# The first expert product by Strassen's scheme, in an attention and mixture-of-experts kernel on one Trainium2 core

## The chip, the core and the metric

The kernel runs on one core of one Trainium2 chip. The core has a matrix engine (TensorE, "PE" in the profile, with its weight loads as "PEld"), a vector engine (DVE), a scalar engine (ACT), GpSimd (POOL) and a queue that issues transfers (SP). TensorE reads its operands from the on-chip memory SBUF and writes to PSUM, an accumulation memory of eight banks of 512 fp32 columns; DVE and ACT read both. Each engine runs its own instructions in the order in which the program emits them, and waits for others through semaphores.

The metric is the device time of one execution in microseconds (us), the median of several runs.

## The reference

The first half is attention over a window of 32 positions (for half of the heads with a dilation of 4). Its output, 4,608 tokens of 512 values, goes through a mixture of experts: each token is sent to its two best of eight experts, and an expert is two matrix products with a ReLU between them.

```python
N, D, E, F = (4608, 512, 8, 1024)
...
for e in range(E):
    for k in range(2):
        mask = top2[:, k] == e
        ...
        h = np.maximum(x[mask] @ w1[e], 0.0)
        out[mask] += top2_w[mask, k, None] * (h @ w2[e])
```

Everything is float32.

## The kernel before, in words

**Attention and routing** (the first 235 us of the profile) are emitted in fixed slots. While they run, each token's row is stored to the scratch tensor `xs`, its two experts are found (`gate`), and POOL scatters the token's number and weight into a table `tab` with one section per expert. Expert 0's section is filled from the start, so that its tokens are available first: `SPLITS` gives the rows that are complete after each quarter of the tokens (384 after the second, 896 after the third).

**Experts.** Each expert has a fixed capacity of 1,152 to 1,216 tokens (`CAPS`), in tiles of 128 (the last one of 64 or 32 tokens, or none). The tiles are grouped into three blocks of 3, 4 and 2 to 3 tiles (`BLS`): 384, 512 and 256 to 320 tokens. For each block, `up` computes the first product, 8 groups of 128 rows of the hidden layer, and `down` the second, tile by tile.

**Precision.** TensorE multiplies float32 operands in a rounded form (`F32R`). Each operand is therefore kept as a high part (its rounding, an ACT cast) and a low part (what is left, a DVE subtraction), and each product is three matmuls: high by high, high by low, low by high. So one row group of `up` is 4 slices of the 512 inputs times 3 = 12 matmuls (line 814) into one PSUM bank, with the block's tokens as the moving columns. After it, ACT takes the ReLU and the high part (L818, `hh`) and DVE the low part (L820, `hl`). A tile of `down` is 8 x 3 = 24 matmuls of 512 columns (L856); DVE scales it (L865, `y`), and POOL adds it to the output rows with an indirect DMA (L833). A last tile of at most 64 tokens is done with its high and low parts stacked in one operand (L850, L852), 16 matmuls.

**Tokens.** A tile's rows are gathered by POOL (four indirect DMAs, L766; two per tile for expert 0, L758), transposed on DVE (L783; for expert 0 on TensorE, L780), cast by ACT (L785) and subtracted by DVE (L786).

**Weights.** `stage_w1` and `stage_w2` load quarters of 512 KB through SP into two staging buffers; `split_w1` and `split_w2` are an ACT cast (L694, L707) and a DVE subtraction (L696, L709).

**The order** of all this work between the matmuls is a plan: `plan(t, f)` notes that `f` is due at time `t`, and `tick(cols)`, called after each group of matmuls, advances a clock by `cols / 2400` us (the columns just emitted) and emits what is due. Since each engine runs in emission order, this places the loads, casts and subtractions between the `hh` and `hl` operations. The order of blocks is written out per expert (first product of block 0, second product of the expert before's block 2, and so on), so that a product always has other work between it and its consumer. `pace()` emits a small POOL copy that waits for a recent `hh`, which holds the gathers behind it back.

## Time and profile before

| | us |
|---|---|
| median of 3 runs | 1053.06 |
| lowest and highest | 1047.64, 1053.71 |
| the profiled execution, first to last instruction | 1109.4 |
| of it, before the first matmul of the first product | 235.7 |
| of it, the eight experts on TensorE | 863.9 |
| of it, after the last matmul | about 10 |

The profile is that of one execution, with the profiler on; it is longer than the runs without it. Its page gives busy times per engine, the chain of waits and the costliest groups of instructions, and the trace behind it can be asked for the instructions of one engine in order of time (start, duration, engine, line, operation, output<-inputs, shape, count, and in brackets the idle time before it and what ended it), for busy times in windows, and for who waited for whom. Matmuls are pipelined: their durations overlap, so what one costs is read from the distance between starts.

### The profile page before, as it was taken

Reading aid. Unit: us, or ns where it says so; the run is one execution under the profiler, and the core shown is the slowest. Engines: PE = TensorE matmul, PEld = TensorE weight load, DVE = VectorE, ACT = ScalarE, POOL = GpSimd, SP = SyncE. Lnnn points to the kernel's source line nnn. Section 1 sums busy time; section 2 is a strip of 40 time slices with the busy share of each in tenths; the row PEclk is TensorE's granted clock in tenths of the full one; section 3 lists DMA queues with packets and bytes.
Section 4 is the critical chain, followed back from the end, with each engine's and each line's share of the span. In section 5 each row is a group of like instructions: output and inputs, shape, how many; then the busy total and the mean of one; then the engine's idle time right before and its main releaser. Section 6 shows DMA issues by size and latency. Waiting matters only on the chain. (4 is left out here: it accounts for less than half of the span.)

```text
span 1109.4 us, 18401 instructions
## 1 busy us (share of the span) xinstructions
PE 1015.0 (91%) x7278; PEld 853.6 (77%) x7279; DVE 463.9 (42%) x1060; ACT 319.8 (29%) x612; POOL 527.7 (48%) x723
## 2 busy tenths in 40 slices
PE   5896776686999899999999999999999999999996
PEld 3774655465779789878988898788978898888885
DVE  6773535644224444334433433434343344333221
ACT  6673433531113232222222222212231213222110
POOL 6004243356866545664635564455456455553112
PEclk9998887887999999999999999999999999999999
DMA  7798687465243432633353334333433443353123
GB/s 275 254 345 292 193 270 251 122 205 161 44 90 76 102 101 48 139 60 103 65 117 68 97 72 101 82 79 85 97 83 81 104 68 102 62 129 58 32 30 46
DMA packets 77530, 132.91 MB, mean 120 GB/s; under 512 B 29968, under 2 KB 39616, under 8 KB 76160
## 3 DMA queue, kind: packets, MB, share of 16 engines
q1 hardware_dynamic: 55088, 92.55, 26.3%
q0 software_dynamic: 22352, 39.15, 19.6%
q8 instruction: 58, 0.95, 0.4%
q14 instruction: 32, 0.26, 0.1%
HBM read 92.11 MB, written 39.54 MB: 119 GB/s over the span
## 5 line engine op out<-in xcount | busy, mean ns | idle before, releaser
L814 PE MATMUL up<-x,w1h 128*128 128x512 f32 (+4 forms) x1536 | 397.5, 345 | 8.8 <-DVE hl L820 5.8
L766 POOL DMA_INDIRECT g<-xs,ixi x258 | 264.5, 1025 | 84.5 <-issue 79.1
L814 PEld LDWEIGHTS up<-x,w1h 128*128 128x128 f32 x1536 | 272.7, 189 | 36.4 <-DVE hl L820 7.6
L814 PE MATMUL up<-x,w1l 128*128 128x384 f32 (+4 forms) x768 | 264.1, 344 | 1.8 <-DVE w1l L696 1.1
L856 PE MATMUL dn<-w2h,hh 128*128 128x512 f32 x576 | 226.7, 394 | 2.0 <-DVE y L865 1.3
L856 PE MATMUL dn<-w2h,hl 128*128 128x512 f32 x576 | 225.3, 391 | 1.1 <-issue 1.1
L856 PE MATMUL dn<-w2l,hh 128*128 128x512 f32 x576 | 225.5, 391 | 0.6 <-issue 0.6
L820 DVE SCALAR_TENSOR_TENSOR hl<-up,hh 128x384 fp32r<-128x384 f32 (+2 forms) x192 | 106.1, 556 | 228.0 <-ACT hh L818 177.1
L833 POOL DMA_INDIRECT out_rows<-y,ixs x67 | 107.8, 1609 | 189.3 <-DVE y L865 158.3
L818 ACT ACTIVATE hh<-up 128x384 fp32r<-128x384 f32 (+4 forms) x192 | 94.2, 498 | 274.7 <-PE up L814 193.9
L814 PEld LDWEIGHTS up<-x,w1l 128*128 128x128 f32 x768 | 145.7, 190 | 14.7 <-DVE w1l L696 1.8
L856 PEld LDWEIGHTS dn<-w2h,hh 128*128 128x128 f32 x576 | 109.0, 189 | 25.6 <-DVE y L865 2.4
L856 PEld LDWEIGHTS dn<-w2h,hl 128*128 128x128 f32 x576 | 108.8, 189 | 24.0 <-issue 1.1
L856 PEld LDWEIGHTS dn<-w2l,hh 128*128 128x128 f32 x576 | 109.0, 189 | 22.6 <-issue 0.8
L865 DVE TENSOR_SCALAR y<-dn,ixs 128x512 f32<-128x512 f32 x63 | 46.9, 748 | 143.4 <-PE dn L856 114.9
L785 ACT CAST x<-xr 128x512 fp32r<-128x512 f32 x67 | 40.5, 605 | 189.9 <-DVE xr L783 158.5
L619 POOL DMA_INDIRECT tab<-en,si x72 | 72.2, 1002 | 30.7 <-issue 16.4
L696 DVE TENSOR_TENSOR w1l<-ws,w1h 128x1024 fp32r<-128x1024 f32 x32 | 38.8, 1217 | 94.8 <-ACT w1h L694 61.6
L297 POOL COPY spacer<-hh 1x1 f32<-1x1 f32 x72 | 24.2, 336 | 102.0 <-ACT hh L818 101.7
L694 ACT CAST w1h<-ws 128x1024 fp32r<-128x1024 f32 x32 | 33.0, 1048 | 115.9 <-DMA ws<-in_moe_w 115.8
L786 DVE TENSOR_TENSOR x<-xr,x 128x512 fp32r<-128x512 f32 x67 | 44.7, 666 | 18.0 <-ACT x L785 15.9
L783 DVE STREAM_TRANSPOSE xr<-g 128x512 f32<-128x512 f32 x67 | 45.7, 682 | 0.0
(184 smaller groups left out, 856.0 us busy)
## 6 DMA issues: line engine op xcount, KB each, us to landing
ws<-in_moe_w SPq DMA_DIRECT2D x64, 512.0 KB
out_rows<-zero SPq DMA_DIRECT2D x38, 256.0 KB
vd<-in_vdl SPq DMA_DIRECT2D x24, 390.0 KB
vp<-in_vpl SPq DMA_DIRECT2D x16, 585.0 KB
qt<-in_qt SPq DMA_DIRECT2D x14, 576.0 KB
xs<-x SPq DMA_DIRECT2D x24, 256.0 KB
kt<-in_kd SPq DMA_DIRECT2D x16, 320.0 KB
g<-xs,ixi POOLq DMA_INDIRECT x258
```

The costliest lines, as they stand in the source:

```text
L619: ins = gpsimd.indirect_dma_start(out=tab, out_offset=bass.IndirectOffsetOnAxis(ap=si[:, kq, t:t + 1], axis=0), in_=en[:, kq, t], in_offse ...
L696: return lambda: vector.tensor_tensor(b, s, a.bitcast(F32), op=OP.subtract)
L766: gpsimd.indirect_dma_start(out=g[:, j], out_offset=None, in_=xq, in_offset=bass.IndirectOffsetOnAxis(ap=IX[e][1][:, r0 // 32 + j:r0 // 32 ...
L783: vector.transpose(xr[:, :, 0:rn].rearrange("p c (g t) -> p g c t", t=32), g[:, 0:n].rearrange("p g (c d) -> p g c d", d=32))
L785: scalar.copy(xh[:, :, o:o + rn], xr[:, :, 0:rn])
L786: return lambda: vector.tensor_tensor(xl[:, :, o:o + rn], xr[:, :, 0:rn], xh[:, :, o:o + rn].bitcast(F32), op=OP.subtract)
L814: tensor.matmul(p[:, 0:n], lhsT=a[:, 128 * f:128 * f + 128], rhs=b[:, kc, 0:n], start=(i == 0), stop=(i == 11))
L818: scalar.activation(hh[:, f, 0:n], p[:, 0:n], AF.Relu)
L820: vector.scalar_tensor_tensor(hl[:, f, 0:m], p[:, 0:m], 0.0, hh[:, f, 0:m].bitcast(F32), op0=OP.max, op1=OP.subtract)
L833: ins = gpsimd.indirect_dma_start(out=out, out_offset=bass.IndirectOffsetOnAxis(ap=sc[0:rn, t, 1:2], axis=0), in_=y[0:rn], in_offset=None, ...
L856: tensor.matmul(p[0:rn], lhsT=a[:, f, o:o + rn], rhs=b[:, f % 2], start=(i == 0), stop=(i == 23))
L865: vector.tensor_scalar(y[0:rn], p[0:rn], wsc, None, op0=OP.mult)
```

## The change

**The scheme.** Both operands of the first product are cut in two in both directions that matter: the 512 inputs into halves, the 1,024 hidden rows into pairs of groups, the block's tokens into halves of each tile. In place of 8 products of blocks, seven are computed, from sums of blocks of weights and sums of blocks of tokens, and the results are put together by additions (Winograd's form). Each product is 2 slices x 3 = 6 matmuls on half of a block's tokens.

**Tokens.** The two halves of each tile's tokens and of its inputs give eight slices, of which four sums are made (`xprep`) before the split: 14 slices of 64 tokens are cast and subtracted per tile (`xsplit`) instead of 4 of 128. Blocks are now two, of `NA = 5` tiles and of the rest (640 tokens, and 512 to 576); there is one buffer for the tokens of a block and one for its hidden layer. `SPLITS` becomes (0, 384, 640).

```diff
-        cuts = [0, 3, 7, len(tl_)]
-        BLS.append([(cuts[i], cuts[i + 1], 128 * cuts[i], min(cap, 128 * cuts[i + 1]) - 128 * cuts[i]) for i in range(3)])
+        BLS.append([(0, NA, 0, 128 * NA), (NA, len(tl_), 128 * NA, cap - 128 * NA)])
...
+    def xprep(e, t):
...
+        vector.tensor_tensor(b[:, 0], q[:, 0, :, 1], q[:, 0, :, 0], op=OP.subtract)
+        vector.tensor_tensor(b[:, 1], q[:, 1, :, 1], b[:, 0], op=OP.subtract)
+        vector.tensor_tensor(b4, q[:, 1, :, 0], b[:, 1], op=OP.subtract)
+        vector.tensor_tensor(q[:, 0, :, 1], q[:, 1, :, 1], q[:, 0, :, 1], op=OP.subtract)
...
+        scalar.copy(a[0], r)
+        def low():
+            vector.tensor_tensor(a[1], r, a[0].bitcast(F32), op=OP.subtract)
```

**Weights.** `kernel()` lays W1 out in blocks, so that one contiguous load of 256 KB brings the four blocks of one pair of row groups `j` and one slice `kk`; a ninth copy holds expert 0's in its other order of inputs. DVE makes four sums of 128 columns from it (`sums_w1`), and ACT and DVE split 7 blocks of 128 columns. W2 comes in eight loads of 256 KB instead of four of 512.

```diff
+    def sums_w1(w, j, kk, eng):
+        s = ST[w, j, kk]
+        a = s[:, 0:512].rearrange("p (i h f) -> p i h f", i=2, h=2)
+        b = s[:, 512:896].rearrange("p (o f) -> p o f", o=3)
+        eng.tensor_tensor(b[:, 0], a[:, 1, 0], a[:, 1, 1], op=OP.add)
+        eng.tensor_tensor(b[:, 1], b[:, 0], a[:, 0, 0], op=OP.subtract)
+        eng.tensor_tensor(b[:, 2], a[:, 0, 1], b[:, 1], op=OP.subtract)
+        eng.tensor_tensor(a[:, 1, 0], a[:, 0, 0], a[:, 1, 0], op=OP.subtract)
...
+        scalar.copy(t[:, 0, :, kk], s)
+        def low():
+            vector.tensor_tensor(t[:, 1, :, kk], s, t[:, 0, :, kk].bitcast(F32), op=OP.subtract)
```

**The first product.** A "row group" `j` is now a pair of 128 rows, and there are four per block. Row group `j`'s products are interleaved with the end of row group `i = j - 1`. `P` is a PSUM bank that accumulates four products in turn, `RQ` a pair of banks; `SU` and `M5` are SBUF copies ("snapshots") of what `P` and `RQ` hold midway, in buffers of their own (pool `ut`).

```diff
+        def mm(p, j, a, b, start):
+            w = W1[e, j]
+            for kk in range(2):
+                for i, (y, z) in enumerate(((0, 0), (0, 1), (1, 0))):
+                    tensor.matmul(p, lhsT=w[:, y, a, kk], rhs=x[:, z, SLOTS[b][kk], 0:N], start=start and kk == 0 and i == 0,
+                                  stop=kk == 1 and i == 2, skip_group_check=True)
+            tick(6 * N)
...
+        for j in range(5):
+            i = j - 1
+            if i >= 0:
+                vector.tensor_tensor(SU[i], SU[i], RQ[i], op=OP.add)
+                high(i, None, SU[i])
+            if j < 4:
...
+                mm(P[j], j, 0, 0, True)
+            else:
+                part()
+            if i >= 0:
+                low(i, None, SU.pop(i))
+            if j < 4:
+                scalar.copy(SU[j][:, 0], P[j])
+            if i >= 0:
+                mm(P[i], i, 2, 2, False)
+                vector.tensor_tensor(M5[i], M5[i], P[i], op=OP.add)
+                high(i + 4, 1, M5[i])
+            if j < 4:
+                mm(RQ[j][:, 1], j, 4, 4, True)
...
+            if i >= 0:
+                low(i + 4, 1, M5.pop(i))
+            if j < 4:
+                scalar.copy(M5[j], RQ[j][:, 1])
+                mm(RQ[j][:, 0], j, 1, 1, True)
+            if i >= 0:
+                mm(P[i], i, 3, 6, False)
...
+                high(i + 4, 0, P[i])
+            if j < 4:
+                mm(P[j], j, 5, 5, False)
...
+            if i >= 0:
+                low(i + 4, 0, P.pop(i))
+            if j < 4:
+                scalar.copy(SU[j][:, 1], P[j])
+                mm(RQ[j][:, 1], j, 6, 3, False)
```

`high` is an ACT ReLU, `low` a DVE subtraction (two for `SU`); for the small last tile each has a further small operation. `part()` emits a quarter of the first tile of the second product.

**The second product** runs block by block right after the first; its scaling moves from DVE to ACT.

```diff
-            vector.tensor_scalar(y[0:rn], p[0:rn], wsc, None, op0=OP.mult)
+            scalar.mul(y[0:rn], p[0:rn], wsc)
```

**The order.** The written plan with due times is replaced by generators that wait for each other: two for weights (one per slice `kk`, each: load, 5.5 us later the sums, 1.5 later the cast once the row group before is done with its buffer, 1.2 later the subtraction), one each for gathers, sums of tokens, splits of tokens and indices. Tokens of a block are split once the first product of the block before has been emitted. Gathers use three buffers instead of four and are preceded by a POOL memset in place of `pace()`.

```diff
+            for j in range(0 if e else 2, 4):
+                stage_w1(EID[e], e, j, kk)
+                yield now[0] + US_LOAD
+                sums_w1(e, j, kk, vector)
+                yield now[0] + 1.5
+                if e:
+                    yield lambda e=e, j=j: free1.get(j, -1) >= e - 1
+                low = split_w1(e, j, kk)
+                yield now[0] + 1.2
+                low()
+                yield now[0] + 0.2
...
     for e in range(E):
...
+        for bi in range(2):
+            t0, t1, _, n = BLS[e][bi]
+            while done.get((e, bi), 0) < t1 - t0:
+                tick(600)
+            begun.add((e, bi))
+            first = down_gen(e, bi, t0)
+            up(e, bi, n, first)
+            down(e, bi, first)
```

For expert 0 the first matmul of the first product comes after all five tiles of its first block have been emitted; its first two pairs of W1 row groups are loaded during attention, as before, and part of its W2 goes through gather buffers (`first_w2`).

More of the change, by code (lines that the diff above doesn't have):

```diff
@@ L257, in setup_c @@
         NR = ET // 16
-        free = [late["stage"].tile([128, FF], I32, name="free", tag="ws") for _ in range(2)]
+        free = [late["stage"].tile([128, 896], I32, name="free", tag="ws") for _ in range(2)]
         pr = free[0][:, 0:3 * NR].rearrange("p (a b) -> p a b", a=3)
@@ new lines, in attention_moe_kernel, with stage_w2, split_w2 @@
+    ready1, ready2 = {}, {}
+    def stage_w2(e, w, f, where=None):
+        s = ST[w, f] = (where or stage)()[:, 0:512]
+        sync.dma_start(s, row(w2, e)[128 * f:128 * f + 128])
+    def split_w2(w, f):
+        s = ST.pop((w, f))
+        a = late["wp2"].tile([128, DM], F32R, name=f"w2h{f}")
+        b = late["wp2"].tile([128, DM], F32R, name=f"w2l{f}")
+        scalar.copy(a, s)
+        def low():
+            vector.tensor_tensor(b, s, a.bitcast(F32), op=OP.subtract)
+            W2[w, f] = (a, b)
+        return low
@@ new lines, in first_w2, with gathers @@
+    def first_w2(fs):
+        held_g[0] += 1
+        for f in fs:
+            stage_w2(0, 0, f, lambda: gp_.tile([128, 4, 128], F32, name="g").rearrange("p a b -> p (a b)"))
+            yield now[0] + US_LOAD
+            low = split_w2(0, f)
+            yield now[0] + 0.9
+            low()
+            yield now[0] + 0.3
+        held_g[0] -= 1
+    def gathers():
+        for e in range(1, E):
+            yield lambda e=e: e in index
+            for t in range(len(TLS[e])):
+                yield lambda: held_g[0] < 3
+                gather(e, t)
+                got[e, t] = now[0]
+                held_g[0] += 1
+                yield now[0] + US_GATHER
@@ new lines, in indices, with rest_of_slots @@
+    def indices():
+        for e in range(1, E):
+            yield lambda e=e: (e - 1, 0) in begun
+            yield now[0] + (42 if e == 1 else 24)
+            new_idx(e)
+            idx_dma(e, 0, CAPS[e])
+            yield now[0] + (12 if e == 1 else 9)
+            idx_copy(e, 0, CAPS[e])
+            index.add(e)
+            yield now[0] + 0.5
+    def rest_of_slots():
+        n = 0
+        while backlog:
+            pace(n % 4 == 0)
+            backlog.pop(0)()
+            n += 1
+            yield 1
@@ new lines, in some_of_slots, with rest @@
+    def some_of_slots():
+        for i in range(min(6, len(backlog))):
+            pace(i == 0)
+            backlog.pop(0)()
+    experts[0] = True
+    for kk in range(2):
+        plan(0.1 + 0.6 * kk, lambda kk=kk: go(weights(kk)))
+    def rest():
+        gens.append(totals())
+        gens.insert(0, first_tiles(NA, len(TLS[0])))
+    gens.append(idx_late(list(gens), SPLITS[2], CAP, rest))
+    for i in range(36):
+        plan(i, some)
+    plan(2.5, some_of_slots)
+    plan(20, lambda: gens.append(rest_of_slots()))
```

437 lines of the change are left out of this document (236 added, 201 removed).

## The prediction

> **What bounds the kernel now.** I read the page's busy shares first, then the busy time of each engine expert by expert (cut where TensorE starts the first product of the next expert), then TensorE's timeline.
>
> ```profile
> span 1109.4 us, 18401 instructions
> PE 1015.0 (91%) x7278; PEld 853.6 (77%) x7279; DVE 463.9 (42%) x1060; ACT 319.8 (29%) x612; POOL 527.7 (48%) x723
> ```
>
> ```profile
> 235.70:365.25 129.55, 117.69 (x563) 99.58 (x562) 49.40 (x161) 25.25 (x47) 86.57 (x129) 0.93 0.46 118
> ...
> 570.12:675.24 105.12, 104.82 (x521) 90.49 (x520) 40.80 (x70) 24.15 (x41) 56.92 (x71) 1.00 0.39 86
> ...
> sum 863.90, PE 841.58 PEld 723.05 DVE 333.74 ACT 197.35 POOL 452.43; mean PE 105.20 PEld 90.38 DVE 41.72 ACT 24.67 POOL 56.55
> ```
>
> The columns after the length are PE, PEld, DVE, ACT and POOL busy, then the granted clock. From 235.70 us to the last matmul the eight experts take 863.90 us, and PE works in 841.58 of them: 22.3 us idle, of which 11.9 lie in expert 0 and 10.5 in experts 1 to 7. So this stage is bound by TensorE's work, at full clock after expert 0, and DVE (41.7 us of some 105 per expert) is cover with room. Busy shares of pipelined matmuls overstate, so I take the price of a matmul from the starts of successive ones:
>
> ```profile
> 601.35 0.63 PE L814 MATMUL up<-x,w1h 128*128 128x512 f32 x2
> ...
> 602.05 0.63 PE L814 MATMUL up<-x,w1h 128*128 128x512 f32 x2
> ...
> 675.24 0.51 PE L814 MATMUL up<-x,w1h 128*128 128x384 f32 x2
> ...
> 675.76 0.51 PE L814 MATMUL up<-x,w1h 128*128 128x384 f32 x2
> ```
>
> ```profile
> 331.12 0.45 PE L814 MATMUL up<-x,w1h 128*128 128x320 f32 x2
> ...
> 331.56 0.46 PE L814 MATMUL up<-x,w1h 128*128 128x320 f32 x2
> ...
> 640.07 0.43 PE L814 MATMUL up<-x,w1h 128*128 128x288 f32 x2
> ...
> 640.47 0.43 PE L814 MATMUL up<-x,w1h 128*128 128x288 f32 x2
> ...
> 852.36 0.40 PE L814 MATMUL up<-x,w1h 128*128 128x256 f32 x2
> 852.60 0.28 PE L814 MATMUL up<-x,w1l 128*128 128x256 f32 x1
> 852.71 0.40 PE L814 MATMUL up<-x,w1h 128*128 128x256 f32 x2
> ```
>
> Three matmuls take 0.70 us at 512 columns, 0.52 at 384, 0.44 at 320, 0.40 at 288, 0.35 at 256: 233, 173, 147, 133 and 117 ns each.
>
> **1. The products.** Before, an expert has 96 matmuls for each of three blocks. For experts 0 to 2: 96 x (173 + 233 + 147) = 53.1 us; for 3 and 4 (third block 288): 51.8; for 5 to 7 (256): 50.2. After, there are two blocks, each 4 row groups x 7 products x 6 matmuls = 168 matmuls of half the block's tokens: 320 columns for the first block, 288, 272 or 256 for the second. These widths are all in the trace (272 lies between two of them, 125 ns). So 168 x (147 + 133) = 47.0, 168 x (147 + 125) = 45.7 and 168 x (147 + 117) = 44.4 us. The saving is 6.1, 6.1 and 5.8 us per expert, 48 us in all: 6 in expert 0 and 42 in the others. That there are 2,688 matmuls where there were 2,304 is already in it. The second product keeps its matmuls: 24 per tile of 128 tokens at 227 ns, 5.4 us; nine tiles and the small last one are some 53 us per expert.
>
> ```profile
> 652.88 0.39 PE L856 MATMUL dn<-w2h,hh 128*128 128x512 f32 x1
> ...
> 653.56 0.39 PE L856 MATMUL dn<-w2h,hh 128*128 128x512 f32 x1
> ```
>
> **2. What DVE and ACT get.** The nearest rows, engine by engine:
>
> ```profile
> L820 DVE SCALAR_TENSOR_TENSOR hl<-up,hh 128x512 fp32r<-128x512 f32 x64 | 44.0, 690 | 96.7 <-ACT hh L818 90.9 <-issue 5.7
> L820 DVE SCALAR_TENSOR_TENSOR hl<-up,hh 128x256 fp32r<-128x256 f32 x64 | 27.0, 423 | 63.6 <-ACT hh L818 51.1 <-issue 12.2
> L862 DVE TENSOR_TENSOR y<-y,dn 64x512 f32<-64x512 f32 x3 | 2.0, 678 | 4.4 <-ACT y L861 4.4
> L786 DVE TENSOR_TENSOR x<-xr,x 128x512 fp32r<-128x512 f32 x63 | 43.3, 687 | 18.0 <-ACT x L785 15.9 <-issue 2.1
> L786 DVE TENSOR_TENSOR x<-xr,x 128x128 fp32r<-128x128 f32 x2 | 0.6, 282 | 0.0
> L783 DVE STREAM_TRANSPOSE xr<-g 128x512 f32<-128x512 f32 x63 | 44.2, 702 | 0.0
> L865 DVE TENSOR_SCALAR y<-dn,ixs 128x512 f32<-128x512 f32 x63 | 46.9, 748 | 143.4 <-PE dn L856 114.9 <-issue 28.5
> L818 ACT ACTIVATE hh<-up 128x512 fp32r<-128x512 f32 x64 | 37.8, 595 | 73.6 <-PE up L814 60.5 <-issue 8.7 <-remote 4.4
> L818 ACT ACTIVATE hh<-up 128x320 fp32r<-128x320 f32 x24 | 10.4, 437 | 45.7 <-PE up L814 29.9 <-issue 15.8
> ```
>
> All are linear: DVE about 150 ns plus 1.05 per column (320: 490 ns; 640: 0.82 us; 896: 1.10 us), ACT 0.83 ns per column (640: 0.70 us).
> DVE per row group: the add of two snapshots 0.82, four low parts 4 x 0.49, one add 0.48, together 3.3 us, so 26 us for the 8 row groups of an expert (13 before). Tokens, per tile: transpose 0.70, four sums of 128 columns 1.13, low part of 14 slices instead of 4 1.10, so 2.93 where it was 1.39; 9.4 tiles give 27.4. W1: 8 x (four sums 1.13 + low part 1.10) = 17.8; W2: 8 x 0.69 = 5.5. The y scaling (9 x 0.75) moves to ACT, where it is about one 0.60 us row and hides between casts. In all DVE goes from 41.7 to about 78 us per expert, of the 98 that PE needs (45.7 and some 53 for the second product). DVE still fits, at 80%, but its cover for PE has become thin. ACT has about 50 us and fits.
>
> Edits with one answer. Weights come in twice as many DMAs of half the size (16 per expert, eight more issues on SP, which idles); a load of twice that size was awaited 3.7 us after its issue, and the new order emits the work on it 5.5 us later (about 6 real ones), so the loads stay hidden. The extra copy of expert 0's W1 is read instead of the plain one, not beside it, and laid out before launch: nothing.
>
> ```profile
> 606.98 3.30 SPq L700 DMA_DIRECT2D ws<-in_moe_w  x2
> ...
> 610.70 1.05 ACT L707 CAST w2h<-ws 128x1024 fp32r<-128x1024 f32 x1 [1.69 <-DMA ws<-in_moe_w]
> ...
> L297 POOL COPY spacer<-hh 1x1 f32<-1x1 f32 x72 | 24.2, 336 | 102.0 <-ACT hh L818 101.7
> ```
>
> The spacer copies on POOL that waited for ACT become memsets that wait for nothing: the gathers behind them on POOL leave earlier and are then held by three gather buffers where there were four. POOL has no wait that ends last in this stage, so I count zero either way.
>
> **3. The new waits inside a product loop.** What follows a product, and how soon:
>
> ```profile
> 641.54 0.30 PE L814 MATMUL up<-x,w1l 128*128 128x288 f32 x1
> ...
> 641.95 0.41 ACT L818 ACTIVATE hh<-up 128x288 fp32r<-128x288 f32 x1 [5.11 <-PE up L814]
> ...
> 642.40 0.42 DVE L820 SCALAR_TENSOR_TENSOR hl<-up,hh 128x256 fp32r<-128x256 f32 x1 [1.38 <-ACT hh L818]
> ```
>
> The last matmul starts at 641.54, the next product could start 0.13 later, and ACT reads 0.28 after that; DVE follows ACT within 0.04. With 320 columns a product is 6 x 0.147 = 0.88 us and a row group of seven 6.16 us. I lay the code's order out from the start of a row group (time 0). TensorE runs A (new snapshot), B (onto the old one), C, D (fresh banks), E (onto the old one), F, G. DVE adds the two banks of the previous row group from 0.27 to 1.09; C and D overwrite these banks from 1.76 on, so 0.7 us are left. ACT takes the high part (1.13 to 1.83); DVE waits for it and does two low parts to about 2.75, then the add that reads B's bank to 3.2; E writes that bank from 3.52 on. So the tightest wait has 0.3 us to spare and the loop by itself costs nothing. At the end of a block the first tile of the second product is emitted in four pieces between the last steps, which fills the waits there; I count 0.5 us per expert.
>
> What costs is other DVE work queued in between: DVE runs in order, and TensorE then waits at E. A piece of work behind A falls into DVE's wait for ACT (0.75 us) and costs nothing up to about 1 us; behind C, D, E or F it falls into gaps of 0.5 to 1.5 us; behind B it delays E by its length less 0.3; two pieces together (the two weight streams run side by side) cost 1 to 2 us behind A, B or G and next to nothing elsewhere. In an expert's first block DVE has 13 us of 24.6 for itself and gets W2's low parts, 5.5 us in four pairs of 1.4: about 0.25 us each, 1.0 us in all. In its second block (22.4 us) it has 13.5 for itself and gets half of W1 (8.9 us in four pairs of about 2.2, at some 0.6 each) and one tile's transpose and sums (1.8 us, at 0.4): 2.8 us, and DVE is full there (24.2 us of durations, which overlap by some 0.07 each). That is 1.0 + 2.8 + 0.5, say 4.5 us per expert. From both sides: at least 1.5 (only what lands behind B), at most 8 (all 10.7 us of the second block's other work pushed out but for the 2 to 3 us that DVE idles beside it, and the first block's pairs at full price). I take 4.5, nearer the lower end, because the row of the same kind, TensorE waiting for DVE's low parts with DVE at 40%, is small:
>
> ```profile
> PE up L814 <- DVE hl L820: 5.8, 5, 2.2
> ```
>
> Experts 1 to 7: 7 x 4.5 = 31.5 us lost. The 10.5 us that stood idle before go: they were DVE evacuating y or hl behind other work and W1 arriving late, in an order that no longer exists; that same work is late next in the waits just counted.
>
> A rule of the Trainium skill bears on this. Its page "TensorE: Matmul & The Clock Gate", section "Back-to-back issue gap", has a warm matmul every N/2.4 ns plus 2.5 ns; the rows here show N/2.4 plus 13 (147 against 133 at 320 columns), so this trace does not agree. By the rule the products would save 46 us instead of 48.
>
> **4. The start of expert 0.** The first block now needs five tiles before its first matmul, not three.
>
> ```profile
> 235.70 0.60 PE L814 MATMUL up<-x,w1h 128*128 128x384 f32 x2
> ...
> 238.32 1.00 POOL L758 DMA_INDIRECT g<-xs,ixf  x1 [6.96 <-DMA ws<-in_moe_w]
> ...
> 242.16 0.96 POOL L758 DMA_INDIRECT g<-xs,ixf  x1 [0.30 <-issue]
> ...
> 253.70 0.20 PE L573 MATMUL posp<-ob,tri 128*128 128x24 bf16 x1 [4.93 <-DVE ob L558]
> ```
>
> TensorE started at 235.70; the gathers of tiles 3 and 4 run from 238.32 to 243.1. I add 2 us of landing, and a copy (0.6), four sums (1.1), cast (0.94) and low part (1.1) behind it: 249, so TensorE stands about 13 us longer. Against that goes expert 0's own idle time of 11.9 us (the gap at 253.70 is the largest): it was spent on TensorE waiting for routing work and late W2, which now runs during the wait. The later tiles of expert 0 are gathered while two tiles fewer are ahead of the routing's scatters on POOL, and their block starts 52 us after 249: covered. Expert 0: 6 (products) + 11.9 - 13.3 - 4.5 (waits as above) = 0. Bounds: -12 (none of the idle time goes) to +8 (tiles 3 and 4 find a free DVE and the waits are few).
>
> **The sum.** 42 + 10.5 - 31.5 + 0 = 21 us less on a profiled execution of 1109.4 us. The median of the runs shown is 1053.06 us, 56 us or 5% below the profiled span; no row shows where these 56 us lie. I take the 21 us as they are: 1032 us.
>
> **The rivals.**
> *Hidden after all.* If the other DVE work lands in the gaps, 1.5 us per expert: 7 x 3 + 3 = 24 us better, 1008 us. For it: the loop has slack at every wait; against it: DVE is full in the second block.
> *DVE becomes the bound (slower).* The place is the second block of each expert, where W1's sums and low parts meet the products. Each microsecond of W1 work that isn't absorbed stops TensorE. The gain of experts 1 to 7 is 52.5 us, so at 7.5 us per expert the time is unchanged; at 10 it is 7 x 5.5 + 5 = 43 us worse than forecast, 1075 us. For it: 78 of 98 us of DVE in an in-order queue with 0.3 us of slack; against it: between the blocks there are some 50 us of second product per expert in which DVE is owed nothing by TensorE and can catch up.
> *The gain is eaten (no change).* Expert 0 loses its 12 us, and the waits cost 6 us per expert: 12 + 7 x 1.5 = 22.5 worse than forecast, 1054 us. For it: the first block's late start is certain, and only what it gives back is open; against it: 11.9 us idle are there to be given back.
> *Shorter matmuls without the profiler.* The runs shown are 56 us shorter than the profiled span, and the two products have some 4,100 matmuls: were each 11 ns shorter in an unprofiled run, that would be 45 of the 56. A product of 320 columns would then last 0.82 us, E would come at 3.26, and the slack there would be 0.06 us. DVE's work stays as long, so each of the 28 row groups in the second blocks of experts 1 to 7 may lose 0.25 us more: 7 us, 1039 us. Against it: no row shows it. The rule quoted above, of the Trainium skill's page "TensorE: Matmul & The Clock Gate", would have it so.
>
> **How the numbers follow.** About 1% (10.5 us) is what a measurement of this kernel can tell from no change. Forecast, waits of 2.5 to 6 us per expert, 1020 to 1042: 0.37. Shorter matmuls, 1030 to 1042: 0.08. Hidden, below 1020: 0.17. Eaten, 1042 to 1064: 0.22. DVE-bound, above 1064: 0.16. So faster 0.62, same 0.22, slower 0.16. For 8 in 10 the range runs from just beyond the hidden case, 1006, to 1070, where the slower one begins in earnest; the likeliest one's own range is 1020 to 1042.
>
> **What would show it.** Right: matmuls of the first product at 147 ns and 2,688 of them; first matmul of expert 0 near 249; expert to expert about 103 us (98 + 4.5) where it was 105 to 109; DVE near 78 us per expert; TensorE's waits for the snapshot adds 20 to 40 us in all, mostly in second blocks. Wrong: these waits above 7.5 us per expert, another spacing at 320 columns, weights or tokens still landing when a block starts (W1's sums waiting on a DMA hold DVE and with it everything), or a first matmul later than 260.

## The result, and the profile after

| | us |
|---|---|
| after, median of 4 runs (lowest to highest) | 1294.24 (1293.17 to 1295.58) |
| before, median of 4 runs beside it | 1052.10 (1047.64 to 1053.71) |
| ratio, 95% interval | 1.2316 (1.2279 to 1.2353) |
| the profiled execution of after, first to last instruction | 1293.8 |

The change makes the kernel 242 us slower; 21 us less was predicted, in a range that ended at 1070. The profiled execution of after lies among its runs. That of before does not, and the profiler is not the reason. The runs of this study were taken in six sets, each with the kernel before beside it: in four sets it takes 1049 to 1053 us (below, chips of the first kind), in two 1115 to 1120 (the second kind). The record numbers the chips of the later sets, and number 6 stands in a set of each kind, so whether the kinds are different chips or states of one isn't shown. The profile shown ahead of the prediction looks like one of the second kind: its span is 1109.4 us, and about a third of its semaphore events are missing (8,878 against 13,452), as in other traces of that kind. Ratios are always to the kernel before of the same set. The kernel before was therefore profiled again on a chip of the first kind (below, `e0_before`; 1049.97 us, span 1048.2 with the profiler on), and after is compared with that.

The page of after, first lines:

```profile
span 1293.8 us, 20803 instructions
PE 1043.0 (81%) x7662; PEld 899.9 (70%) x7663; DVE 698.9 (54%) x1828; ACT 505.4 (39%) x1010; POOL 523.2 (40%) x723
```

Busy time by stretches, cut where expert 0's and expert 1's first products start and at the last matmul: length, then PE, PEld, DVE, ACT, POOL, then the granted clock. First the kernel before on the chip of the first kind, then after:

```profile
194.54:310.18 115.64, 111.87 (x563) 96.36 (x562) 50.01 (x161) 25.55 (x47) 86.97 (x128) 0.99 0.50 133
310.18:1038.60 728.42, 723.08 (x3593) 623.54 (x3591) 284.77 (x453) 172.39 (x289) 367.53 (x455) 1.00 0.40 83
```

```profile
216.91:360.57 143.66, 119.39 (x592) 104.80 (x593) 85.62 (x247) 54.56 (x105) 76.78 (x111) 0.87 0.35 83
360.57:1284.20 923.63, 759.62 (x3929) 667.66 (x3927) 467.83 (x1062) 321.61 (x617) 359.95 (x454) 0.91 0.32 66
```

Of the 245.6 us between the two ends (1284.20 against 1038.60), 22.4 are the later start, 28.0 the longer expert 0, and 195.2 experts 1 to 7: 132 us each where it was 104. In experts 1 to 7 PE stands idle for 164 us (923.63 - 759.62) where it stood for 5.3, and its clock falls from 1.00 to 0.91. What PE waited for in after (sum, times, longest):

```profile
PE urq L854 <- ACT m L917: 129.1, 64, 6.0
PE dn L968 <- ACT w2h L726: 29.0, 9, 6.9
PE dn L968 <- DVE w2l L729: 21.1, 9, 4.7
...
PE urq L854 <- DVE su L889: 1.6, 1, 1.6
...
PE upg L854 <- DVE m L908: 1.0, 2, 0.5
...
PE up L854 <- DVE m L908: 0.7, 1, 0.7
```

The wait at E for DVE's add, the one the prediction watched, is in the last two of these lines (E's bank is called `up` or `upg`): 1.7 us in the whole run. The first line has 64 waits, one for each of 8 experts x 2 blocks x 4 row groups: product D waits for ACT's copy of the snapshot M5. One of them, in the timeline of PE, ACT and DVE (start, duration, idle time before):

```profile
709.14 0.92 PE L854 MATMUL urq<-x,w 128*128 128x272 f32 x6
...
710.10 0.43 DVE L908 TENSOR_TENSOR m<-m,up 128x272 f32<-128x272 f32 x1
710.27 0.39 ACT L905 COPY su<-upg 128x272 f32<-128x272 f32 x1 [0.87 <-DVE h L879]
710.56 0.42 ACT L870 ACTIVATE h<-m 128x256 fp32r<-128x256 f32 x1
...
711.01 0.43 DVE L876 SCALAR_TENSOR_TENSOR h<-m,h 128x256 fp32r<-128x256 f32 x1 [0.48 <-ACT h L870]
711.35 0.17 DVE L879 SCALAR_TENSOR_TENSOR h<-m,h 128x16 fp32r<-128x16 f32 x1
...
711.61 0.39 ACT L917 COPY m<-urq 128x272 f32<-128x272 f32 x1 [0.53 <-DVE h L879]
...
712.05 1.02 PE L854 MATMUL urq<-x,w 128*128 128x272 f32 x6 [1.98 <-ACT m L917]
712.90 0.92 PE L854 MATMUL up<-x,w 128*128 128x272 f32 x6
713.65 0.91 PE L854 MATMUL upg<-x,w 128*128 128x272 f32 x6
714.41 0.92 PE L854 MATMUL urq<-x,w 128*128 128x272 f32 x6
```

C is the six matmuls at 709.14. D follows at 712.05, though it writes the other bank of the pair: the pair is one tile, the copy (L917) reads C's half of it, and the program makes D wait for that read. The copy itself cannot start before DVE has read the old M5, which has one buffer (the low parts at 711.01 and 711.35), and these stand behind ACT's high part and DVE's add. So the whole chain of DVE and ACT for one snapshot lies between C and D. Of the 64 waits, 26 last 1.87 to 2.07 us, as this one does, and 15 some 0.5 to 0.8 (nearly all in the first row group of a block, where no old M5 is still to be read). The 21 of 2.29 us and more add up to 67: other DVE work stands in or just ahead of the chain in all of them, for instance at 452.07 us two low parts of W1 (2.09 us together) ahead of the add, and D waits 4.32 us. The last lines also show what was right: a product of 272 columns starts every 0.755 us, 126 ns a matmul, where 125 was counted.

A wait can cost more than its length. In expert 1:

```profile
373.47 1.97 PE L854 MATMUL urq<-x,w 128*128 128x320 f32 x6 [3.07 <-ACT m L917]
375.23 1.81 PE L854 MATMUL up<-x,w 128*128 128x320 f32 x6
376.83 1.81 PE L854 MATMUL upg<-x,w 128*128 128x320 f32 x6
378.43 1.50 PE L854 MATMUL urq<-x,w 128*128 128x320 f32 x6
```

After a pause of 3.07 us six matmuls take 1.76 us, twice the 0.88 counted, and three products and most of a fourth pass before the speed is back; the granted clock is 0.50 from 373.47 to 379.4 us. The Trainium skill's page "TensorE: Matmul & The Clock Gate", section "What's actually happening", has the clock fall to half after an idle window of about 3.4 us and rise again after a busy one. This trace agrees on the half; the recovery, some 6 us, lies between one and two such windows, and a pause of 3.07 us was already enough. The length of the pause alone does not decide: in after a pause of 1.99 us (ending at 392.96) is followed by 3.4 us at a clock of 0.52, while many pauses of that length are followed by a clock of 1.00, and in `k1_shared` (below) one of 3.01 us (ending at 822.42) keeps it at 1.00.

The second cost is at the end of each first block, where the first tile of the second product needs W2's last pieces (expert 2):

```profile
538.93 0.49 PE L968 MATMUL dn<-w2h,h 128*128 128x512 f32 x1 [1.33 <-ACT w2h L726]
...
543.42 1.29 DVE L729 TENSOR_TENSOR w2l<-ws,w2h 128x512 fp32r<-128x512 f32 x2
544.16 0.80 PE L968 MATMUL dn<-w2l,h 128*128 128x512 f32 x1 [4.74 <-DVE w2l L729]
```

### The profile page after: what moved, and what is told of

The parts are those of the page before. It is cut to its first block, busy times and chain, and to the rows that moved or that the text cites. A ratio compares the mean times of both kernels' runs of the same rounds, so it can differ in the third digit from the quotient of the medians.

```text
span 1293.8 us, 20803 instructions
## 1 busy us (share of the span) xinstructions
PE 1043.0 (81%) x7662; PEld 899.9 (70%) x7663; DVE 698.9 (54%) x1828; ACT 505.4 (39%) x1010; POOL 523.2 (40%) x723
## 4 chain that ended last, share of the span: by engine, by line
PE 32%; issue 24%; DVE 13%; POOL 11%; ACT 6%; DMA 2%; POOLq 0%; DVEq 0%; ACTq 0%; SPq 0%
PE dn L968 15%; PE urq L854 7%; POOL g L788 6%; PE up L854 5%; POOL out_rows L943 4%; PE upg L854 3%; DVE h L876 2%; DVE x L829 2%; ACT h L870 2%; DVE w L712 2%; DVE su L889 1%; DVE xr L809 1%; ACT m L917 1%; DVE w2l L729 1%; PE o L405 1%
## 5 line engine op out<-in xcount | busy, mean ns | idle before, releaser
L968 PE MATMUL dn<-w2h,h 128*128 128x512 f32 x1152 | 378.7, 402 | 30.1 <-ACT w2h L726 29.0
L854 PE MATMUL urq<-x,w 128*128 128x320 f32 (+3 forms) x1152 | 215.2, 327 | 130.7 <-ACT m L917 129.1
L854 PEld LDWEIGHTS urq<-x,w 128*128 128x128 f32 x1152 | 184.8, 209 | 146.7 <-ACT m L917 144.6
L968 PEld LDWEIGHTS dn<-w2h,h 128*128 128x128 f32 x1152 | 224.3, 195 | 79.9 <-ACT w2h L726 32.5
L968 PE MATMUL dn<-w2l,h 128*128 128x512 f32 x576 | 232.5, 404 | 21.1 <-DVE w2l L729 21.1
L854 PE MATMUL up<-x,w 128*128 128x320 f32 (+3 forms) x864 | 165.2, 336 | 11.2 <-ACT x L826 5.8
L854 PEld LDWEIGHTS up<-x,w 128*128 128x128 f32 x864 | 149.2, 222 | 15.5 <-ACT x L826 5.9
L968 PEld LDWEIGHTS dn<-w2l,h 128*128 128x128 f32 x576 | 112.2, 195 | 46.5 <-DVE w2l L729 24.7
L854 PE MATMUL upg<-x,w 128*128 128x320 f32 (+3 forms) x672 | 124.7, 327 | 1.0 <-DVE m L908 1.0
L854 PEld LDWEIGHTS upg<-x,w 128*128 128x128 f32 x672 | 113.3, 216 | 4.3 <-DVE m L908 2.4
```

Source lines behind the costliest of these rows:

```text
L854: tensor.matmul(p, lhsT=w[:, y, a, kk], rhs=x[:, z, SLOTS[b][kk], 0:N], start=start and kk == 0 and i == 0, stop=kk == 1 and i == 2, skip_ ...
L968: tensor.matmul(p[0:rn], lhsT=h[:, a, f, r0:r0 + rn], rhs=b, start=(i == 0), stop=(i == 23), skip_group_check=True)
```

## The experiments

**Theory A**: the shared tile costs most of the loss, by its waits and by the clock that they lower; late W2 pieces cost the next part. **Rival B**: the chain of DVE and ACT is the bound, and without the wait at D it is felt elsewhere. **Rival C**: W2 is late only because the loop is slow.

### D ahead of C, and the tile cut in two (second kind of chip)

`e1_swap`:

```diff
-                mm(RQ[j][:, 1], j, 4, 4, True)
+                mm(RQ[j][:, 0], j, 1, 1, True)
...
+                mm(RQ[j][:, 1], j, 4, 4, True)
                 scalar.copy(M5[j], RQ[j][:, 1])
-                mm(RQ[j][:, 0], j, 1, 1, True)
```

> Product D (into the first half of the two-bank snapshot tile) is issued ahead of product C (into its second half); ACT's copy of the second half stays right behind C. Nothing else moves. Theory A (TensorE stands at D because the tile is tracked as a whole: D writes only the half that the copy does not read, yet waits for that copy, which is queued on ACT behind a wait for DVE): the row urq <- ACT m L917, 129 us in the changed kernel, falls below 15 us, the mean granted clock rises from 0.905 to 0.95 or more, and the time from 1294 to about 1080 to 1120 us. Rival B (the chain of DVE and ACT itself is the bound, and the wait only shows where it is felt): TensorE's idle time moves to the products behind DVE's adds or to the next row group, and the time stays above 1250 us.

`e2_tiles`:

```diff
-                vector.tensor_tensor(SU[i], SU[i], RQ[i], op=OP.add)
+                for z in range(2):
+                    vector.tensor_tensor(SU[i][:, z], SU[i][:, z], RQ[i][z], op=OP.add)
...
-                RQ[j] = late["mps"].tile([128, 2, 512], F32, name="urq", tag="urq", bufs=1)[:, :, 0:N]
+                RQ[j] = [late["mps"].tile([128, 512], F32, name=f"urq{z}", tag=f"urq{z}", bufs=1)[:, 0:N] for z in range(2)]
```

> The order of the products stays as in the changed kernel, but the two snapshot halves are two tiles of one bank each, so that a write to one does not wait for a read of the other. Price: DVE's add of two halves at 820 ns becomes two adds of about 480 ns, 0.14 us more per row group. Theory A (the shared tile is the cause): time within 15 us of the run with D and C exchanged, waits on ACT m gone, 1080 to 1130 us. Rival B (DVE and ACT are the bound): above 1250 us. A second rival, that the exchange helps by its order and not by what it stops waiting for: this one stays near 1290 us while the exchange is fast.

This set came from a chip of the second kind, so the times of after could not be laid beside it, and after was run again in the next set, which was of that kind too:

> The changed kernel again, beside the others, because the four runs so far had a kernel before of 1115 us instead of 1052, with idle stretches of 2 to 6 us that the waits put down to nothing ("issue", "remote"). If the chip that this call gets is like that one: about 1350 us, ratio near 1.22, and the exchange of D and C was worth some 75 us. If the changed kernel takes 1294 us where the kernel before takes 1115, the exchange was worth 16 us only and theory A falls with it. If the chip is like the first one: 1294 us and 1.23.

| | us | ratio to before (95%) |
|---|---|---|
| `c_after` | 1432.03 | 1.2791 (1.2738 to 1.2845) |
| `e1_swap` | 1277.88 | 1.1461 (1.1427 to 1.1495) |
| `e2_tiles` | 1271.86 | 1.1418 (1.1377 to 1.1460) |

Both edits take away the wait, in different ways (3.9 and 5.2 us are left of it), and gain nearly the same against `c_after` of the other set, 154 and 160 us. That the order alone would help is out, since the tiles keep it. By their times both stand above the 1250 us that were expected under rival B, and some waits do appear behind DVE's adds (for `m`, 30.1 us in `e1_swap`); on this kind of chip rival B could not be judged. The absolute times expected were wrong, because on this chip every kernel is slower, and after more than the kernel before (1432 against 1294, a thing I had expected at 1350). In the profile of `c_after` TensorE stands for up to 11 us with no recorded releaser (sum, times, longest):

```profile
PE urq L854 <- ACT m L917: 140.7, 54, 8.6
PE urq L854 <- issue: 52.0, 11, 11.3
PE dn L968 <- ACT w2h L726: 28.9, 9, 6.9
```

What these stretches are stays open; about a third of the semaphore events are missing from these traces (10,091 against 15,942), so that some of the waits put down to "issue" have a cause that was not recorded. What follows uses chips of the first kind wherever it can.

### The late W2 pieces (second kind of chip)

`e3_early`, and `e4_both` (it and the exchange):

```diff
-                yield lambda e=e: (e - 1, 1) in begun
+                yield lambda e=e: len(EID) > e and (e - 1, 0) in begun
```

> The snapshots stay as in the changed kernel; only the condition that lets the next expert's first-layer weights into the queue is met half an expert earlier, so that the loads of the second-layer weights, which stand in the same queue, come earlier too. Theory (late second-layer weights cost on their own): the waits of the second product for ACT w2h L726 and DVE w2l L729, 50 us together, fall below 15 us, and the time falls by 35 to 60 us, to 1235 to 1260 us. Rival C (their lateness is only what the slow product loop leaves of DVE and ACT): the waits stay at 35 us or more, time 1280 us or more.

> Exchange of D and C and earlier loads together. Theory A with late weights as a cause of their own: 1020 to 1055 us, about or under the kernel before (1052 us), granted clock near 0.97 or more. If lateness of the second-layer weights is only a consequence of the waits at D (rival C): within 15 us of the exchange alone. If DVE and ACT are the bound (rival B): above 1200 us.

`e3_early` took 1400.29 us, 1.2550 (1.2502 to 1.2598); `e4_both` 1274.83, 1.1410 (1.1363 to 1.1457). Both missed: the waits for w2h and w2l fell only from 50 to 45 us. In the code a piece of W2 cannot be split before the expert before is done with its buffer, so the condition that I moved need not be the one that binds. `e3_early` is 0.024 below `c_after`, more than these waits give; that is a comparison between two sets, and beside the exchange, in the same set, the edit brought 0.005, within the intervals. The pieces come one after the other in two streams, four each, each with its load, cast and low part. So the next edit shortened what the plan allows for a load:

```diff
-US_LOAD = 5.5
+US_LOAD = 3.8
```

> Two snapshot tiles, and the time that the planner allows for a load of weights cut from 5.5 to 3.8 us (the loads land 3.7 us after their issue). Theory (second-layer weights are late because each of the two streams loads, waits, splits four tiles one after the other where it had two of double size before): the waits for w2h and w2l fall from 50 us to 20 or less and the ratio to the kernel before by 0.03 to 0.05 from the 1.142 of the two tiles alone. Rival (they wait for DVE's queue, not for their loads): waits 40 us or more, ratio above 1.125.

`f1_load` (with the two tiles): 1263.12 us, 1.1296 (1.1247 to 1.1346). Now the waits for W2 are gone entirely, but the ratio fell by 0.012 only, where 0.03 to 0.05 was expected: the waits for DVE's add grew in their place (PE for DVE m, up and upg together: 63.3 us in 34 waits, 19.9 in `e2_tiles`). How much it is worth was seen only on the other kind of chip, below.

### The order of DVE's work, and places for other work (second kind of chip)

`f2_order`, beside the two edits before it:

```diff
-            if i >= 0:
-                low(i, None, SU.pop(i))
-            if j < 4:
-                scalar.copy(SU[j][:, 0], P[j])
             if i >= 0:
                 mm(P[i], i, 2, 2, False)
                 vector.tensor_tensor(M5[i], M5[i], P[i], op=OP.add)
                 high(i + 4, 1, M5[i])
+                low(i, None, SU.pop(i))
+            if j < 4:
+                scalar.copy(SU[j][:, 0], P[j])
```

> As the run before it, and in the product loop DVE's add for the snapshot M5 and ACT's high part of it go ahead of DVE's two low parts of the sums, which raises the slack at product E from some 0.3 to some 1.1 us (ACT's copy of the first product moves behind them, still 0.6 us ahead of its need). Theory B (the order of DVE and ACT within a row group is a bound of its own once the shared tile is gone): waits for m L909 fall below 8 us from about 20, ratio lower by 0.01 to 0.02. Rival (what is left is other work queued in between and stalls without a semaphore): ratio within 0.005 of the run before.

1244.46 us, 1.1127 (1.1058 to 1.1195): the gain expected, 0.017, but the waits for m fell only from 63.3 to 49.7 us, where less than 8 was expected, so the reason given for it isn't shown. `f3_places` lets `mm` only advance the plan's clock, and emits what is due ahead of E and ahead of G:

```diff
-            tick(6 * N)
+            now[0] += 6 * N / 2400.0
...
                 mm(RQ[j][0], j, 1, 1, True)
+            tick(0)
...
                 low(i + 4, 0, P.pop(i))
+            tick(0)
```

> As the run before it, and other work (splits and sums of weights and tokens) is queued at two places of a row group only, ahead of E and ahead of G, where DVE would stand, not behind every product. Theory of the prediction (what is queued in between costs): ratio lower by 0.01 to 0.03, and no wait for m over 1 us. Rival (the pieces only gather at these places and delay the sums behind G instead): no gain, waits of urq for su instead of m.

1332.23 us, 1.1892 (1.1837 to 1.1947), a miss: each step of a stream (load, cast, low part) could leave only at a place, so W2 was late again (PE dn for w2h 38.4 us, for w2l 22.8).

### Pacing and places on a chip of the first kind

`g1_pace` is `f2_order` with POOL's gathers held behind ACT, as the kernel before had it:

```diff
                 high(i, None, SU[i])
+                late["h"] = late["yt"].tile([1, 1], F32, name="pc", tag="pc", bufs=6)
+                scalar.copy(late["h"], SU[i][0:1, 0, 0:1])
...
-            gpsimd.memset(spacer, 0.0)
+            gpsimd.tensor_copy(spacer, late["h"])
```

`g2_places` is `f2_order` in which only DVE's pieces wait for a place; `here(1)` stands where `f3_places` had `tick(0)`, and `place` is true for one piece there, and always outside the loop. `g3_pace_places` has both.

```diff
                 yield now[0] + US_LOAD
+                yield place
                 sums_w1(e, j, kk, vector)
...
                 yield now[0] + 0.9
+                yield place
                 low()
```

> As the run with two tiles, short loads and the add ahead (ratio 1.113), and the gathers on POOL are paced again as in the kernel before: ahead of the four gathers of a tile POOL reads one element that ACT wrote in the current row group (an ACT copy of one element per row group, some 0.2 us), where the change had put a write that waits for nothing. Theory G (gathers that run back to back on POOL hold up the others: the idle stretches of 2 to 8 us that the profile puts down to nothing fall where POOL works without a break): waits without a releaser on DVE and ACT fall by half, ratio 1.04 to 1.09. Rival (pacing is without effect, as the prediction counted it): ratio 1.10 to 1.12.

> As the run with two tiles, short loads and the add ahead (ratio 1.113), and inside the product loop each DVE piece of other work (sums, low parts, transposes of tokens) waits for one of two places of a row group, one piece at each; everything else goes on as before, so that the loads are not held back as in the earlier try with places (1.189). Theory (other work ahead of DVE's adds is what still stops TensorE at E): waits for m below 15 us instead of 49, ratio 1.06 to 1.10, and waits for w2h and w2l stay below 10 us. Rival (the waits at m are the chip's own stalls, not work queued ahead): ratio within 0.01 of 1.113.

> Pacing and places together. If both theories hold their gains add: ratio 1.00 to 1.05. If only one holds, within 0.01 of that run alone.

`g1_pace` 1066.43 us, 1.0161 (1.0107 to 1.0214); `g2_places` 1097.71, 1.0456 (1.0389 to 1.0523); `g3_pace_places` 1097.19, 1.0461 (1.0412 to 1.0509). Since the kind of chip had changed, the first of these could not be read as a gain by pacing; the second and third differ by less than their intervals, so pacing is worth nothing that shows here. With places, the second blocks of experts 1 to 4 ran at 47 to 48 us, but first blocks at 61 to 65, with 39 us of waits for W2.

### The shares, one after the other (first kind of chip)

> The kernel before, profiled beside the others. If the chip is like the first one (kernel before 1049 to 1053 us): the experts start near 200 us instead of 235.7, and take 840 to 845 us together instead of 864, almost none of it idle; then the 10.5 us of idle time that the prediction let go in experts 1 to 7 were the chip's, not the kernel's, and no gain was to be had there. If the experts take 860 us or more here too, the prediction's account of the kernel before stands.

> The snapshot as two tiles, nothing else changed, as the run of 1.142. On a chip like the first one: theory A (the shared tile is nearly all of the loss): 1090 to 1120 us, ratio 1.04 to 1.07, waits for ACT's copy gone, waits for w2h and w2l still 40 to 50 us. If the late second-layer weights and DVE's order weigh as much as the tile: 1150 us or more, ratio above 1.10.

> Two tiles, loads planned at 3.8 us, DVE's add ahead of its low parts, as the run of 1.113, and without the pacing of gathers. If pacing is without effect (as places with and without it, 1.046 both, suggest): within 0.01 of 1.016, the run that had it. If pacing was what brought 1.016: 1.05 or more. Against the two tiles alone it shows what the late weights and the order cost on this chip: 30 to 60 us by theory A.

`h1_second` is `g2_places` with places in second blocks only:

```diff
+        grant[0] = 0 if bi else 99
```

> As the run beside it, with places for other DVE work in second blocks only (the first blocks, which need their second-layer weights soon, take it as it comes). From the earlier runs on a chip like the first: first blocks at 52 us and second blocks at 47.5 instead of 51, so 3.5 us less for each of seven experts, 25 us in all: ratio 0.985 to 1.0. If the weights of the next expert then come late: waits for w L709 and L712 at the start of experts and 1.01 or more.

| | us | ratio to before (95%) | step |
|---|---|---|---|
| after (its own runs) | 1294.24 | 1.2316 (1.2279 to 1.2353) | |
| `e2_again`: two tiles | 1134.46 | 1.0808 (1.0749 to 1.0868) | -160 |
| `f2_again`: and short loads, add ahead | 1065.69 | 1.0157 (1.0101 to 1.0212) | -69 |
| `h1_second`: and places in second blocks | 1047.59 | 0.9971 (0.9944 to 0.9998) | -18 |

`e0_before` came out as expected for the first kind: the experts start at 194.54 us and take 844.06, of which 9.1 are idle. Two tiles came out slower than theory A had it (1090 to 1120), with all 50 us of W2's waits still in, so rival C falls; the loads and the order then gave 69 us, more than expected. `f2_again` (1.0157) and `g1_pace` (1.0161) agree within their intervals, which again shows no effect of pacing. The first step compares two sets, whose kernels before took 1052.10 and 1051.5 us. W2's waits are absent from `f2_again`, and PE's stretches are

```profile
211.96:334.20 122.24, 110.82 (x592) 95.02 (x593) 85.18 (x256) 54.73 (x107) 78.14 (x112) 0.97 0.44 105
334.20:1048.70 714.50, 695.62 (x3929) 614.67 (x3927) 466.24 (x1117) 319.02 (x615) 374.50 (x453) 1.00 0.40 84
```

for `f2_again`, and for `h1_second`

```profile
215.77:332.95 117.18, 109.00 (x592) 95.55 (x592) 82.96 (x253) 54.33 (x106) 78.04 (x110) 0.96 0.42 101
332.95:1036.90 703.95, 690.62 (x3928) 615.92 (x3928) 468.07 (x1120) 320.79 (x617) 372.57 (x455) 0.99 0.42 86
```

With these edits the scheme comes near to what the prediction meant: experts 1 to 7 in 714.5 and 703.95 us where the kernel before takes 728.42, full clock, DVE as busy as in after (466 and 468 us against 467.83). So DVE's load was not the bound, and rival B falls but for some 20 us of waits in `e2_again` (below). Nearly all of what `h1_second` gains in experts 1 to 7, 24.5 us, goes to expert 1's start, 332.95 where it was 310.18.

### The last three

`h2_two` grants two pieces at the first of the two places (`here(2)`); `h3_half` also adds the first half of the snapshots early:

```diff
-                for z in range(2):
-                    vector.tensor_tensor(SU[i][:, z], SU[i][:, z], RQ[i][z], op=OP.add)
+                vector.tensor_tensor(SU[i][:, 1], SU[i][:, 1], RQ[i][1], op=OP.add)
...
                 low(i + 4, 0, P.pop(i))
+            if j < 4:
+                vector.tensor_tensor(SU[j][:, 0], SU[j][:, 0], RQ[j][0], op=OP.add)
```

`k1_shared` is `h2_two` with the pair of banks one tile again, that is, with the diff of `e2_tiles` undone.

> As the run with places in second blocks (0.997), but two pieces at the first of the two places, so that expert 6's last second-layer weight, for which TensorE waited 4.2 us there and ran at half speed behind it, is split in time. Expected: that block 53 us instead of 63.6, ratio 0.985 to 0.992. If two pieces at one place delay the adds instead: waits for m above 5 us and 0.997 or more.

> As the run beside it, and DVE adds the first half of the two snapshots at the second place, before the last product of the row group, so that only the other half is left behind that product. It frees 0.5 us of DVE's chain, which no wait above 0.5 us in second blocks shows to be on TensorE's path: ratio within 0.004 of the run beside it; in first blocks up to 0.5 us per row group could be had, 0.985 at best.

> As the first run of this call, with the two snapshot tiles made one again. Theory A: D waits again for ACT's copy, some 1.5 us in each of 64 row groups: waits of 80 to 110 us for ACT m, the granted clock down to 0.93 or less by the pauses, ratio 1.08 to 1.15. If the tile costs only together with late weights and the old order of DVE's work: ratio below 1.03.

`h2_two` 1057.14 us, 1.0069 (1.0044 to 1.0094), a miss: the late weight is gone, but other waits came, for DVE's add of the snapshots (8.7 us in 6 waits of up to 1.5) and for ACT's copy (9.6 us). Two pieces at one place would explain them; that isn't shown. `h3_half` 1058.41, 1.0082 (1.0057 to 1.0108): no effect, as expected. `k1_shared` 1163.75, 1.1108 (1.1052 to 1.1164): putting the shared tile back costs 107 us, as theory A had it (the granted clock, 0.953, fell less than expected), with one wait in each row group again (sum, times, longest):

```profile
PE urq L868 <- ACT m L933: 105.5, 64, 5.3
```

So two thirds of the tile's cost don't hang on late weights or on the old order: 160 us taken away from the changed kernel, 107 put back into one where DVE's add comes ahead and the weights are in time. The shares fit the traces. From first product to last matmul PE has the same 4,520 matmuls; with two tiles in place of one (`e2_again` against after) its idle time falls from 188.3 to 84.7 us and its busy time from 879.0 to 822.9, by 104 and 56. With the tile put back (`k1_shared` against `h2_two`) idle time rises from 32.3 to 111.2 us and busy time from 801.3 to 826.8, by 79 and 26. That the same matmuls take longer fits the lower granted clock.

## Why the prediction was wrong

**The matmuls** (48 us saved by the products): the price was right, 126 ns at 272 columns against 125, and so was their number. The formula that the prediction sets beside it is given on the Trainium skill's page "TensorE: Matmul & The Clock Gate", section "Back-to-back issue gap", for an isolated matmul.

**DVE's load**: 78 us per expert was predicted (the terms listed add up to 77), 69 measured (553.45 us in the eight), and it is no bound, as predicted.

**The loop by itself costs nothing**: this is the step that failed. The layout gave "C, D (fresh banks)" and watched the reads of the row group before, and E. It left out one instruction in the code, ACT's copy of C's bank into M5, and its two conditions: the pair of banks is one tile, so D waits for the copy, and M5 has one buffer, so the copy waits for DVE's low part of the old one. With the same figures the timeline goes on: the add ends at 3.2, ACT's high part takes it to 3.7, DVE's low part to 4.2, the copy to 4.6; D was laid out at 2.64. That is 2.0 us per row group, and 26 of the 64 waits are of this size. That their average, 129.1 / 64 = 2.0, is the same is partly chance, since the short waits of first row groups and the long ones behind other DVE work even out. The rows to see it were there; the dependency wasn't drawn. Splitting the tile removed the first condition; a second buffer for M5 alone was not tried. The other work that the prediction saw queued on DVE behind B did cost time, but at D. The 160 us that go with the tile are more than these 129 us, although some 20 us of other waits came in their place in `e2_again` (for DVE's m 13.5, ACT's m 5.7, DVE's su 4.2): 104 us are idle time and 56 are matmuls that run faster, with the granted clock up from 0.905 to 0.943.

**The loads stay hidden**: failed, by 50 us of waits, 69 us of time together with the order of DVE's work. The bytes were not the point, since `f2_again` loads the same without such a wait. What took these waits away was the allowance of 3.8 us in place of 5.5 for each piece of a serial stream (`f1_load`: 50 us of waits before, none after). That the larger number of pieces made it matter is an argument; no run changed it. How the 69 us divide between loads and order was not measured on this kind of chip.

**Full clock**: taken over from the kernel before without a reason; 0.905 was granted over the run.

**4.5 us per expert lost to work queued on DVE** (bounds 1.5 to 8): in the changed kernel the 21 long waits at D hold 25 us beyond 2.0 us each (67 - 42), some 3 us per expert. Once the other two are gone a remainder of this size is left: experts 1 to 7 of the kernel before less 42 us of products are 686; `f2_again` takes 28 us more, 4.0 per expert, `h1_second` 18, 2.5. Not all of it is shown to be waiting, since PE idles there for 18.9 and 13.3 us, and both have an order of DVE's work that the prediction did not have; so how near the agreement is, is partly luck.

**10.5 us idle in the kernel before, to be had**: about half wrong. On a chip of the kind that the timed runs had, its experts 1 to 7 idle for 5.3 us (728.42 - 723.08); the rest, and the 56 us that no row explained, went with the profiled execution, since `e0_before` has a span of 1048.2 us.

**Expert 0 comes out even**: failed. The start is 22 us later where 13 was counted, and the kernel before has only 3.8 us of idle time in expert 0 to give back (115.64 - 111.87), not 11.9; even in `f2_again` expert 1 starts 24 us later. This takes about all that the scheme gains, which is why the mended kernel ends level with the one before. The 9 us beyond the 13 counted can be read from the traces. First `e0_before`, then after, the last gather of expert 0's tiles 3 and 4 and what follows it:

```profile
201.24 0.96 POOL L758 DMA_INDIRECT g<-xs,ixf  x1 [0.30 <-issue]
```

```profile
206.20 0.95 POOL L780 DMA_INDIRECT g<-xs,ixf  x1 [0.30 <-issue]
...
212.89 1.09 DVE L829 TENSOR_TENSOR x<-xr,x 128x896 fp32r<-128x896 f32 x1 [1.06 <-ACT x L826]
...
214.07 0.59 ACT L807 COPY xr<-xrp 128x512 f32<-128x512 f32 x1 [1.21 <-DVE x L829]
...
216.91 0.63 PE L854 MATMUL up<-x,w 128*128 128x320 f32 x1 [5.84 <-ACT x L826]
```

The gathers end 5.0 us later. From their end to the first matmul it takes 9.8 us where some 6 were counted, because the second tile's copy waits for the first one's low part: two tiles pass one after the other, and one was counted.

**The rivals.** The slower one, DVE as the bound at W1's work in second blocks, didn't occur: the loss is in every row group of every block, and DVE is at 69 us of 133 per expert. *Shorter matmuls without the profiler* falls too: `e0_before` was profiled, took 1049.97 us, and three matmuls of 384 columns take the same 0.52 us there (310.18 to 310.70). None of the rivals had this wait.

## What to carry to other kernels

When a new buffer is written in halves, draw for each writer all readers of the whole tile, as the program tracks it, and follow each copy into its engine's queue and to the last reader of its destination; here two tiles cost one more short add on DVE, one tile 2.0 us of TensorE, 64 times. Where loads are steps of a serial stream, count what is allowed for each one times their number: here 1.7 us less per piece took 50 us of waits to none. Before idle time in a profile is counted as gain, see that the profile's span fits the timed runs; here it was 56 us above them.

## What the runs showed of the hardware

A pause of TensorE can halve its speed for some us behind it (one of 3.07 us for 6 us, one of 1.99 us for 3.4), so that waits spread over a loop cost more than their sum: with 129 us of them taken away and some 20 us of others come, idle time fell by 104 us and the same matmuls ran 56 us faster. Not every pause did so: one of 3.01 us left the clock at 1.00. One and the same kernel differs between sets of runs by more than most changes are worth: the kernel before took 1049 to 1053 us in four sets and 1115 to 1120 in two, and the ratio of one and the same change was 1.23 on the first kind of chip and 1.28 on the second.
